# Causal block attention with a gated convolution: loads from two queues at the start, transposes evacuated between the two normalisations, the gates' work spread over the steps

## The chip, the core and the metric

One NeuronCore of a Trainium2 chip runs the whole kernel. The metric is device time in microseconds; the median of three runs stands for a kernel. Instructions run on five engines with a queue each: PE (TensorE, matmuls and transposes), DVE (VectorE), ACT (ScalarE), POOL (GpSimd) and SP (SyncE, which here only issues DMAs). ACT's queue issues some DMAs too.

## What is computed

Attention over 8 batches and 8 heads, 576 positions, head size 64, with a mask in blocks of 64 positions: a query sees its own block and all blocks before it. Its output, heads side by side (512 channels), goes through a gated unit: a causal convolution over 5 positions, per channel, gives the gate.

```python
scores = (q @ k.T) / sqrt(64)                  # masked by blocks of 64
attn   = softmax(scores) @ v                   # B, H, S, D
x      = attn, heads side by side              # B, S, 512
gate   = sigmoid(sum over k of conv_w[k] * xp[:, k:k+S])   # xp: x with 4 zeros ahead
out    = (gate * (x @ w_val)) @ w_out
```

## The kernel before

The 64 heads are worked in 32 pairs, p = 0 to 31; p belongs to batch b = p // 4. One trip of the loop at line 430 is called a step. The order of instructions on each engine is the order of the program: nothing is rescheduled (`tc.manual_schedule()`), and the framework only adds the waits.

A step p does, in the order of the program:

- **loads(p)**, line 388: on SP, q and k of pair p+4 (`load_qk1`), v of pair p+3 (`load_v1`), in some steps the last 64 positions ("tails") of q and k of a coming batch (`load_tails`) and of v (`load_vtail`), and in steps 1 to 4 the halves of w_val and w_out. The staging tiles of q, k and v have 4 buffers each.
- **casts(p)**, line 405: POOL turns float32 into float16: q and k of pair p+1 (from p = 5 on of pair p+2 as well, one step ahead), v of pair p, the tails, and in p = 6 and 7 the halves of w_out (`cast_w_out`).
- **s_tile(p, 0)** and **(p, 1)**, line 168: score matmuls into PSUM tiles S (two buffers), then exp on ACT into `pt`.
- **av(p-1)**, line 213: for each of the pair's two heads, 15 matmuls of the probabilities of the pair before with v into one PSUM bank, then on DVE a reciprocal of the sums (L234) and a multiplication (L235), which write `x16`.
- **trans(p+1)**, line 148: 8 transposes of the next pair's q and k on PE into bank 2, and one DVE copy to SBUF (`qkT`, L165).
- `permute_w_out` in p = 8 (two of them), 9 and 10, or an output tile from p = 11 on (`out(3)`: 4 matmuls of 512 columns in bank 3, a copy, a DMA).
- **s_tile(p, 2)** (here called S2) with its exp, and **mask(p)** (L204, L206): POOL writes zeros into the masked parts of `pt`. av(p) of the next step needs it.
- `s_last`, the scores among the tails, in some steps.
- from p = 5 on, with gs = p - 5: in even gs **conv(gs // 2)**, line 251, 80 small matmuls into one S tile and banks 0 and 1, then tanh on ACT (L266 for the two G banks, then L268 for the S tile).
- **xtrans(p-1)**, line 239: 5 transposes of `x16`, one DVE copy to `xts` (L246).
- in p = 5 and 6, two times `scale_w_val` (DVE, L379).
- from p = 6 on, two calls of **val**, line 271: 4 matmuls of x with w_val, then a DVE operation that applies the gate (`gv`, L282). The first uses bank 3, the second bank 0 or 2.
- `trans_tails` in some steps (PE, and a DVE copy L144).

[...] two S tiles of two banks each, and four single banks G0 to G3, which are given out by number. A bank is written again only when its last reader is done.

Step p = 0 is different: nothing is there to be normalised, and dummy matmuls (`warm(n)`, zeros by zeros) stand between the parts. Before the loop, the first loads, constants, the casts and the transposes of pair 0 are issued.

After the loop, the last av, the last val and conv and the output tiles that are left follow. Of the 36 output tiles, 21 are computed in steps 11 to 31 and 15 after the loop. In the tail, an output tile and a val alternate on PE.

Of the kernel before, what the change touches and what calls it, by code (L numbers as in the profile page):

```python
# [10 lines left out]
def kernel(  # L11
# [10 lines left out]
    nc = tc.nc  # L22
# [68 lines left out]
    def load_tails(b):  # L91
        t = p2.tile([128, 8, 64], fp32, tag="tlst", name="tlst")
        tl_st[b] = t
        for o, src in ((0, q), (64, k)):
            nc.sync.dma_start(out=t[o:o + 64, 0:8, 0:64],
                              in_=src[b, 0:8, 512:576, 0:64].rearrange("h s d -> s h d"))
# [5 lines left out]
    def load_v1(p):  # L102
        b, g = divmod(p, 4)
        t = p4.tile([128, 4, 2, 64], fp32, tag="vs1", name="vs1")
        for h in range(2):
            nc.sync.dma_start(
# [13 lines left out]
    def cast_qk(p, first=False):  # L120
# [4 lines left out]
        if first:  # L125
            nc.scalar.copy(out=o[:, 0:2], in_=s[:, 0:2])
# [86 lines left out]
    def av(p, banks):  # L213
# [3 lines left out]
        x = p2.tile([128, 5, 2, 64], fp16, tag="x16", name="x16")  # L217
        x16[p] = x
        for h in range(2):
            r = gbank(banks[h])  # L220
            for i in range(5):
                for j in range(i + 1):
                    if j == 4:
                        o = 64 * (4 * h + g)
                        l = pt4[b % 2][0:128].rearrange("p a s -> p (a s)")[:, o:o + 128]
                        w = v16t[b % 2][0:128, 2 * g + h, 0:65]
                    else:
                        o = 1280 + 64 * j if i == 4 else off[j] + 128 * i
                        l = pt[0:128, h, o:o + 128]
                        w = vv[0:128, j, h, 0:65]  # L230
                    mm(r[0:128, 65 * i:65 * i + 65], l, w, start=(j == 0), stop=(j == i))
            O = r[0:128, 0:325].rearrange("p (i d) -> p i d", d=65)
            rc = p2.tile([128, 5, 1], fp32, tag="rc", name="rc")
            nc.vector.reciprocal(out=rc[0:128], in_=O[:, :, 64:65])  # L234
            nc.vector.tensor_tensor(  # L235
                out=x[0:128, 0:5, h, 0:64], in0=O[:, :, 0:64],
                in1=rc[0:128].to_broadcast([128, 5, 64]), op=ALU.mult)
# [13 lines left out]
    def conv(n, banks=(None, None)):  # L251
# [13 lines left out]
        for row in (2, 3):  # L265
            nc.scalar.activation(out=t[0:128, row, 0:288], in_=rr[row][:, 0:288],  # L266
                                 func=AF.Tanh, bias=0.0, scale=0.5)
        nc.scalar.activation(out=t[0:128, 0:2, 0:288], in_=s[0:128, 0:2, 0:288],  # L268
# [119 lines left out]
    def loads(p):  # L388
        b, m = divmod(p, 4)
        if b + 2 < B and m == 2:  # L390
            load_tails(b + 2)
# [137 lines left out]
```

The softmax here doesn't subtract the row's maximum and nothing guards it: scores larger than these inputs give would overflow.

## Time and profile before

| | us |
|---|---|
| runs (three) | 198.04, 198.52, 198.67 |
| median | 198.52 |
| the profiled execution, its own time | 198.43 |
| its span in the trace | 196.6 |
| PE busy | 183.3 (93%) |
| DVE busy | 130.8 (67%) |
| ACT busy | 138.6 (71%) |
| POOL busy | 83.5 (42%) |

Times within the trace count from the start of the span. A step is found in the timeline by its score matmuls: the first ones of p = 1 start at 14.26 us, of p = 2 at 18.00, p = 3 at 21.74, p = 4 at 25.48, p = 6 at 34.27, p = 7 at 39.86, p = 8 at 46.32, p = 9 at 52.10, p = 10 at 57.19, p = 11 at 61.58, p = 12 at 67.19 and p = 13 at 72.10. In a timeline each line is: start in us, duration in us, engine, source line, operation, output<-input, shapes, count, and in brackets how long the engine had been idle and what ended that. A matmul's duration includes its way through the array, so that neighbours overlap; the distance between starts is what PE spends. In the view by windows each line has the window, its length, then busy time (and instructions) of PE, PEld (weight loads), DVE, ACT and POOL, the granted clock, the busy share of the DMA engines (above 1 when packets overlap) and GB/s.

### The profile page before, as it was taken

Reading aid. Unit: us, or ns where it says so; the run is one execution under the profiler, and the core shown is the slowest. Engines: PE = TensorE matmul, PEld = TensorE weight load, DVE = VectorE, ACT = ScalarE, POOL = GpSimd, SP = SyncE. Lnnn points to the kernel's source line nnn. Section 1 sums busy time; section 2 is a strip of 40 time slices with the busy share of each in tenths; the row PEclk is TensorE's granted clock in tenths of the full one; section 3 lists DMA queues with packets and bytes.
Section 4 is the critical chain, followed back from the end, with each engine's and each line's share of the span. In section 5 each row is a group of like instructions: output and inputs, shape, how many; then the busy total and the mean of one; then the engine's idle time right before and its main releaser. Section 6 shows DMA issues by size and latency. Waiting matters only on the chain.

```text
span 196.6 us, 8730 instructions
## 1 busy us (share of the span) xinstructions
PE 183.3 (93%) x3714; PEld 124.4 (63%) x3714; DVE 130.8 (67%) x286; ACT 138.6 (71%) x192; POOL 83.5 (42%) x168
## 2 busy tenths in 40 slices
PE   2999878779899999999999999999999999999992
PEld 1456656557577676667766677677767676755550
DVE  4346785897678686777686877768676868642451
ACT  4438778758699778877888878887988787635321
POOL 7363664596444554345434644464445422100000
PEclk9999999999999999999999999999999999999998
DMA  5999999999899568876887687977775111124445
GB/s 155 256 286 265 250 274 323 312 215 278 242 224 253 171 174 217 255 228 186 236 232 234 189 240 212 276 216 207 220 213 146 57 56 58 58 107 165 163 160 213
DMA packets 70337, 40.43 MB, mean 206 GB/s; under 512 B 48149, under 2 KB 64789, under 8 KB 70298
## 3 DMA queue, kind: packets, MB, share of 16 engines
q1 hardware_dynamic: 69872, 39.46, 73.8%
q8 instruction: 29, 0.48, 1.0%
q10 hardware_dynamic: 426, 0.40, 0.6%
q14 instruction: 10, 0.08, 0.2%
HBM read 30.42 MB, written 9.44 MB: 203 GB/s over the span
## 4 chain that ended last, share of the span: by engine, by line
PE 80%; DVE 10%; POOL 3%; ACT 2%; DMA 2%; issue 1%; POOLq 0%; SPq 0%; DVEq 0%; ACTq 0%
PE G L33 51%; PE S L33 18%; PE G L154 6%; PE G L244 5%; DVE qkT L165 3%; DVE x L235 3%; DMA vs<-in_v_dram 2%; POOL qk L129 1%; ACT pt L188 1%; PE G L141 1%; DVE w_val L379 1%; DVE rc L234 1%; DVE gv L282 1%; POOL v L134 1%; POOL pt L204 1%
## 5 line engine op out<-in xcount | busy, mean ns | idle before, releaser
L188 ACT ACTIVATE pt<-S 128x1024 f16<-128x1024 f32 x96 | 95.0, 1024 | 21.4 <-PE S L33 19.1
L204 POOL MEMSET pt<- 64x384 f16 x32 | 13.5, 423 | 74.0 <-ACT pt L188 73.9
L33 PE MATMUL G<-xt,w_val 128*128 128x288 f16 x256 | 37.9, 286 | 0.3 <-DVE qkT L165 0.2
L165 DVE COPY qkT<-G 128x1024 f16<-128x1024 f16 x31 | 37.7, 1215 | 0.2 <-PE G L154 0.2
L129 POOL CAST qk<-qks 128x1024 f16<-128x1024 f32 x31 | 32.9, 1061 | 10.9 <-DMA qks<-in_k_dram 7.7
L33 PEld LDWEIGHTS <-pt 128*128 128x128 f16 x960 | 31.2, 97 | 8.6 <-issue 4.0
L33 PE MATMUL G<-w_out,gv 128*128 128x512 f16 x144 | 36.5, 379 | 0.0
L33 PE MATMUL G<-v,pt 128*128 128x65 f16 x896 | 34.1, 194 | 1.7 <-DVE gv L282 1.3
L282 DVE SCALAR_TENSOR_TENSOR gv<-th,G 128x288 f16<-128x288 f32 x64 | 28.2, 453 | 10.7 <-PE G L33 9.0
L304 ACT COPY osb<-G 128x512 f32<-128x512 f32 x31 | 18.2, 586 | 23.8 <-PE G L33 22.0
L235 DVE TENSOR_TENSOR x<-G,rc 128x320 f16<-128x320 f32 x64 | 31.5, 492 | 2.2
L33 PEld LDWEIGHTS <-qkT 64*128 64x128 f16 x496 | 16.0, 94 | 22.9 <-issue 16.8
L33 PE MATMUL S<-qkT 64*128 64x512 f16 (+1 forms) x248 | 28.5, 301 | 2.1 <-DVE qkT L165 1.1
L33 PEld LDWEIGHTS <-w_val 128*128 128x128 f16 x256 | 24.2, 98 | 8.5 <-issue 0.9
L234 DVE RECIPROCAL rc<-G 128x5 f32<-128x5 f32 x64 | 12.2, 190 | 22.6 <-PE G L33 22.5
L246 DVE COPY xt<-G 128x576 f16<-128x576 f16 x32 | 14.6, 455 | 13.5 <-PE G L244 13.2
L154 PE MATMUL G<-ident,qk 128*128 128x128 f16 x256 | 20.1, 222 | 0.2 <-POOL qk L129 0.2
L134 POOL CAST v<-vs 128x512 f16<-128x512 f32 x32 | 19.9, 621 | 0.5 <-DMA vs<-in_v_dram 0.3
L33 PEld LDWEIGHTS <-gv 128*128 128x128 f16 x144 | 12.9, 98 | 9.9
L33 PE MATMUL G<-xt,DG 32*32 32x288 f16 x640 | 17.2, 288 | 0.0
L33 PE MATMUL S<-xt,DG 32*32 32x288 f16 x640 | 17.1, 287 | 0.0
L154 PEld LDWEIGHTS <-qk 128*128 128x128 f16 x256 | 15.4, 100 | 1.3 <-POOL qk L129 0.4
(58 smaller groups left out, 151.8 us busy)
## 6 DMA issues: line engine op xcount, KB each, us to landing
out_dram<-osb SPq DMA_DIRECT2D x35, 256.0 KB, 2.1
qks<-in_q_dram SPq DMA_DIRECT2D x32, 256.0 KB, 4.2
vs<-in_v_dram SPq DMA_DIRECT2D x64, 128.0 KB, 4.4
qks<-in_k_dram SPq DMA_DIRECT2D x31, 256.0 KB, 4.3
tlst<-in_q_dram SPq DMA_DIRECT2D x8, 128.0 KB, 4.8
tlst<-in_k_dram SPq DMA_DIRECT2D x8, 128.0 KB, 4.6
vtst<-in_v_dram SPq DMA_DIRECT2D x8, 128.0 KB, 4.8
w_st<-in_moe_w_val_dram SPq DMA_DIRECT2D x2, 512.0 KB, 6.3
```

Source lines behind the costliest of these rows:

```text
L33: nc.tensor.matmul(out=out, lhsT=lhsT, rhs=rhs, start=start, stop=stop, skip_group_check=True)
L129: nc.gpsimd.tensor_copy(out=o, in_=s)
L134: nc.gpsimd.tensor_copy(out=v16s[p % NV][0:128, 0:4, 0:2, 0:64], in_=s)
L154: nc.tensor.transpose(out=r[:, o:o + 128], in_=t[0:128, c, 2 * i:2 * i + 2, 0:64], identity=ident16[0:128, 0:128])
L165: nc.vector.tensor_copy(out=o[0:128].rearrange("p i (s n) -> p i s n", n=4), in_=src)
L188: nc.scalar.activation(out=pts[p % NPT][0:128, 0:2, 512 * t:512 * t + 512], in_=s[0:128, 0:2, 0:512], func=AF.Exp, bias=0.0, scale=0.125)
L204: nc.gpsimd.memset(pt[64:128, 0:2, 0:1536].rearrange("p h (t s) -> p h t s", t=3)[:, :, :, 0:64], 0.0)
L234: nc.vector.reciprocal(out=rc[0:128], in_=O[:, :, 64:65])
L235: nc.vector.tensor_tensor(out=x[0:128, 0:5, h, 0:64], in0=O[:, :, 0:64], in1=rc[0:128].to_broadcast([128, 5, 64]), op=ALU.mult)
L246: nc.vector.tensor_copy(out=xts[b % NX][0:128, g, 4:4 + SEQ], in_=r[:, 0:SEQ])
L282: nc.vector.scalar_tensor_tensor(out=gv[u][0:128, x, bi, hf, 0:288], in0=t[0:128, x, 0:288], scalar=1.0, in1=r[0:128, 0:288], op0=ALU.add, ...
L304: nc.scalar.copy(out=o[0:128], in_=r[0:128, 0:512])
```

## The change

Start. `load_tails(0)` and `load_v1(0)` are issued right behind the first q and k; the k part of the tails and both DMAs of v(0) go to ACT's DMA queue. `conv_nat` goes from ACT's queue to SP's, behind v(2). The first cast of q moves from ACT to DVE. The zeros for the dummy matmuls are written earlier.

Steps 0 to 4 get a loop of their own. Step 0 has fewer dummies and does trans(1) right after S2(0); conv_weights moves to p = 2. In steps 1 to 4 the transposes of `x16` are done two pairs behind instead of one, ahead of av (`x16` gets three buffers), and the program has the normalisation of head 0, av of head 1, trans(p+1), then the normalisation of head 1, so that DVE's copy of `qkT` stands between the two normalisations.

Loads and casts. The q and k tails of batch 2 are loaded in p = 4, behind v(7), instead of in p = 2 ahead of pair 6; they are cast and transposed in p = 6 instead of 4. `s_last(2)` goes from p = 6 to p = 8. The casts of w_out stand behind the mask in p = 7 and 8 instead of ahead of it in p = 6 and 7.

Gates. For p < 13 ("early") there is no output tile; the first val of a step takes its place, ahead of S2, and both val use bank 3. All four `scale_w_val` are in p = 6, two ahead of the first val and two after xtrans. The four `permute_w_out` are at the end of p = 9, 10, 11 and 12, in bank 2. In early steps conv's tanh takes the S tile first. Output tiles begin with p = 13.

```diff
         for o, src in ((0, q), (64, k)):
-            nc.sync.dma_start(out=t[o:o + 64, 0:8, 0:64],
+            (nc.scalar if b == 0 and o else nc.sync).dma_start(
+                              out=t[o:o + 64, 0:8, 0:64],
...
-    def load_v1(p):
+    def load_v1(p, eng=None):
...
         if first:
-            nc.scalar.copy(out=o[:, 0:2], in_=s[:, 0:2])
+            nc.vector.tensor_copy(out=o[:, 0:2], in_=s[:, 0:2])
             nc.vector.tensor_copy(out=o[:, 2:4], in_=s[:, 2:4])
...
-    def av(p, banks):
+    def av(p, h, bank):
...
+    def norm(p, h, bank):
+        if h == 0:
+            x16[p] = p3.tile([128, 5, 2, 64], fp16, tag="x16", name="x16")
+        O = GT[bank][0:128, 0:325].rearrange("p (i d) -> p i d", d=65)
+        rc = p2.tile([128, 5, 1], fp32, tag="rc", name="rc")
+        nc.vector.reciprocal(out=rc[0:128], in_=O[:, :, 64:65])
+        nc.vector.tensor_tensor(
+            out=x16[p][0:128, 0:5, h, 0:64], in0=O[:, :, 0:64],
+            in1=rc[0:128].to_broadcast([128, 5, 64]), op=ALU.mult)
+
+    def avs(p, banks):
         for h in range(2):
...
+            av(p, h, banks[h])
+            norm(p, h, banks[h])
...
-        for row in (2, 3):
...
+        for part in ((0, 2, 3) if score_first else (2, 3, 0)):
...
     load_qk1(0)
+    load_tails(0)
+    load_v1(0, nc.scalar)
...
-    nc.scalar.dma_start(out=conv_nat[0:5, 0:512], in_=moe_conv_w[:, :])
-    load_tails(0)
     make_identity(nc, ident)
+    wz = const([128, 512], fp16, "wz")
+    nc.vector.memset(wz[0:128], 0.0)
...
     load_v1(2)
+    nc.sync.dma_start(out=conv_nat[0:5, 0:512], in_=moe_conv_w[:, :])
...
-        if b + 2 < B and m == 2:
+        if b + 2 < B and m == 2 and b > 0:
             load_tails(b + 2)
...
-        if p == 0:
-            load_tails(1)
+        if p in (0, 4):
+            load_tails(1 + p // 4)
...
+    def tails(p):
+        if p in (3, 6):
+            return p // 3
+        return p // 4 + 1 if p > 4 and p % 4 == 0 and p + 4 < NP else None
...
-        if p in (6, 7):
-            cast_w_out(p - 6)
+        if tails(p):
+            cast_tails(tails(p), nc.gpsimd)
...
+    for p in range(LAG):
         loads(p)
         casts(p)
         s_tile(p, 0)
         s_tile(p, 1)
         if p == 0:
-            warm(3)
+            warm(2)
             trans_tails(0, 0)
...
+            s_tile(0, 2)
+            mask(0)
+            trans(1, 2)
+            warm(2)
+            s_last(0)
+            warm(4, 3)
+            continue
+        if p > 1:
+            xtrans(p - 2, 3)
+        av(p - 1, 0, 0)
+        norm(p - 1, 0, 0)
+        av(p - 1, 1, 1)
+        trans(p + 1, 2)
+        norm(p - 1, 1, 1)
         s_tile(p, 2)
         mask(p)
+        if p == 1:
+            warm(2, 3)
+        if p == 2:
+            conv_weights()
+        if tails(p):
+            trans_tails(tails(p), 0)
+        if p == 4:
+            s_last(1)
+
+    for p in range(LAG, NP):
+        gs = p - LAG
+        cv = gs % 2 == 0
+        early = p < 13
+        h = gs - 1
+        loads(p)
+        casts(p)
+        s_tile(p, 0)
+        s_tile(p, 1)
+        if p == LAG:
+            xtrans(p - 2, 3)
+        avs(p - 1, (0, 1) if cv else (1, 0))
+        if p < NP - 1:
+            trans(p + 1, 2)
+        if p == 6:
+            scale_w_val(0)
+            scale_w_val(1)
+        if not early:
+            out(3)
+        elif gs > 0:
+            val(h // 2, 2 * (h % 2), 3)
+        s_tile(p, 2)
+        mask(p)
+        if p in (7, 8):
+            cast_w_out(p - 7)
+        if p == 8 or (p % 4 == 2 and p > 6 and p + 2 < NP):
             s_last((p + 2) // 4)
...
         if cv:
-            conv(gs // 2, (0, 1))
...
+            conv(gs // 2, (0, 1), early)
+        xtrans(p - 1, 2 if cv else 0)
+        if p == 6:
+            scale_w_val(2)
+            scale_w_val(3)
         if gs > 0:
...
+            if not early:
+                val(h // 2, 2 * (h % 2), 3)
+            val(h // 2, 2 * (h % 2) + 1, 3 if early else 0 if cv else 2)
             if h % 2 == 1:
                 complete(h // 2)
-        if p == 8:
-            permute_w_out(1, 1)
...
+        if 9 <= p <= 12:
+            permute_w_out(p - 9, 2)
+        if tails(p):
+            trans_tails(tails(p), 1)
```

## The prediction

> **What bounds the kernel now.** I read four views in this order: the page's slices, busy time by windows, the timelines of POOL, DVE and PE one engine at a time, and the landing times of single DMAs. The page shows where there is room.
>
> ```profile
> PE   2999878779899999999999999999999999999992
> DMA  5999999999899568876887687977775111124445
> ```
>
> A slice is 4.9 us. PE is full from the twelfth slice on: the last 140 us only repeat what PE has to do, and a change pays only if PE is further ahead when this stretch begins. DMA is full in slices 2 to 9, exactly where PE has its gaps. The windows say the same with numbers:
>
> ```profile
> 8.00:12.00 4.00, 4.00 (x38) 2.29 (x33) 0.64 (x3) 2.96 (x3) 2.68 (x5) 1.00 1.20 251
> ...
> 28.00:32.00 4.00, 3.12 (x70) 2.29 (x67) 2.53 (x6) 3.29 (x4) 2.60 (x5) 1.00 1.12 323
> 32.00:36.00 4.00, 3.09 (x110) 1.88 (x107) 3.44 (x7) 3.34 (x7) 2.38 (x4) 1.00 1.09 316
> ...
> 40.00:44.00 4.00, 2.70 (x82) 1.99 (x86) 3.58 (x9) 2.20 (x3) 3.75 (x6) 1.00 0.89 198
> ```
>
> The columns are PE, PEld, DVE, ACT, POOL, clock, DMA share, GB/s. A DMA share above 1.0 from 3 to 40 us means a backlog: loads land in the order of issue, as fast as the engines allow. "PE 4.00" in 8 to 12 us is largely warm-up filler (11 of p=0's 16 dummy matmuls). What the backlog does is in POOL's timeline:
>
> ```profile
> 30.15 1.04 POOL L129 CAST qk<-qks 128x1024 f16<-128x1024 f32 x1
> 33.56 1.04 POOL L129 CAST qk<-qks 128x1024 f16<-128x1024 f32 x1 [2.37 <-DMA qks<-in_k_dram]
> 34.55 0.62 POOL L134 CAST v<-vs 128x512 f16<-128x512 f32 x1
> 35.23 0.57 POOL L204 MEMSET pt<- 64x384 f16 x1
> ...
> 38.30 1.04 POOL L129 CAST qk<-qks 128x1024 f16<-128x1024 f32 x1 [2.08 <-DMA qks<-in_k_dram]
> ```
>
> This is step p=5: the casts of pairs 6 and 7, then v, then the mask, in one queue. Pair 7 is wanted only in step 6, but POOL stands 2.37 us for it, and av(5) waits for the mask behind it (PE resumes at 35.85). Steps 5 to 7 thus already run at the pace of the loads. Later, DVE's order counts; step p=10:
>
> ```profile
> 58.46 0.20 DVE L234 RECIPROCAL rc<-G 128x5 f32<-128x5 f32 x1 [0.71 <-PE G L33]
> ...
> 59.73 1.22 DVE L165 COPY qkT<-G 128x1024 f16<-128x1024 f16 x1
> 60.86 0.45 DVE L246 COPY xt<-G 128x576 f16<-128x576 f16 x1
> 61.22 0.92 DVE L282 SCALAR_TENSOR_TENSOR gv<-th,G 128x288 f16<-128x288 f32 x2
> ```
>
> With av(9) starting at 57.73, the qkT evacuation ends at 60.95: 3.2 us after the start of av, in every step.
>
> **What the Trainium skill says.** "DMA: Bandwidth & Descriptors", section "Issuing engines are not separate DMA queues": loads issued from several engines run on the same 16 DMA engines and interleave, and a second queue saves only the sequencer's issue time. The shares above 1.0 agree that the engines, not SP, are short. "PSUM — Partial Sum Buffer", "PSUM bank collisions raise a hardware error": two engines may not be on one bank at once, so a bank is handed over only when its reader is done. The trace agrees: DVE's L160 stood 1.8 us for ACT's L159 on the other half of the same bank. "TensorE: Matmul & The Clock Gate", Part 1: the clock is halved until some 3.4 us of activity. The first four warm-up matmuls took 1.89 us, three at 8.18 us only 0.82, which agrees.
>
> **Part 1, the start (p=0).** q on DVE instead of ACT: DVE's half (0.43) can run while k is awaited (4.68), the ACT cast (0.62) goes; wz is cleared earlier, so the warm-ups no longer stand ahead of trans(0). S(0) comes about 0.5 earlier (7.63 now). The three DMAs moved to ACT's queue (k tail, two of v) free 1.8 us of issue on SP (0.62 + 1.21) and let vtail and pair 2 be issued earlier, which a full DMA gives no faster; conv_nat, 10 KB, goes to SP behind v(2), long ahead of its use in p=2. Bytes ahead of pair 1 grow by up to v(0) (256 KB, 0.9 us at 280 GB/s), so the cast of pair 1 (7.86 now) moves by 0 to +1.2. trans(1) follows it at once instead of standing at 12.31 behind conv_weights (1.05 us) and 11 dummies. Cast at 9.0, trans 10.1, qkT copy (1.23) to 12.0: S(1) at 11 to 12 instead of 14.26. **Lead 2.2 to 3.3 us**, with the clock perhaps still halved in part of it.
>
> **Part 2, steps 1 to 4.** Moving qkT ahead of the second normalisation frees it 0.63 us (L234+L235), but trans ends only 0.65 after av, and xtrans (0.31) now stands before av: DVE's loop S, av, qkT stays at 0.54+0.31+0.92+0.65+1.22 = 3.65 us against 3.74. It does not bind alone: S2, exp (0.51+1.03), mask (0.66), cast of q and k (1.10), trans (0.55) closes at 3.85 to 3.9 us (S2 at 16.27, 20.12, 23.97, 27.88), on PE, ACT and POOL, and is not touched. **Gain 0 to 0.1 a step; I take 0.** conv_weights in p=2 costs 1.05 us on PE and 1.0 on DVE, in their 0.8 us of slack a step: at most 0.3, taken as 0. The tanh order costs nothing by itself: the S bank comes free 0.7 earlier, row 3 as much later, and av of the next step waits up to 0.2 for it (a term below).
>
> **Part 3, loads and casts.** On SP the q and k of tails(2) move from ahead of pair 6 to behind v(7). By single landings, w_val lands at 19.61+7.0 = 26.6, the tails at 28.2: 1.6 us of DMA (their bytes alone at 250 GB/s would be 1.05, the low end). Pair 7's k, now 27.63+5.8 = 33.4, lands at 31.8. POOL: cast to 32.9, v to 33.5, mask to 34.1; av(5) at 34.05 instead of 35.85. **This is where the lead of part 1 is handed back**: whatever steps 0 to 4 gained, POOL waits for pair 7, and 1.8 us remain. Moved past each other on POOL: the cast of tails(2) (0.62) goes from p=4 to p=6, ahead of mask(6); its load, now behind v(7), lands at about 38.9, the cast ends at 39.5, before mask(6) is due (S2(6) at 38.4 plus 2.15). The casts of w_out (1.24, 1.05) leave their place ahead of mask(6) and mask(7), which was 41.14 and 44.88, for one behind mask(7) and mask(8); what waits behind them there, the cast of pair 10, has a step to spare. s_last(2) (0.21 on PE, 0.6 on ACT) goes from p=6 to p=8, with the same slack.
>
> **Part 4, step 6.** Before, two of the four scalings of w_val ran at 34.75 in DVE's idle time. Now all four are in p=6, and val(0,0) stands on PE before S2(6). DVE after av(5): first rc at 34.8, both normalisations 1.27, qkT 1.2, scale 0.67: PE waits until 37.9, S2(6) is at 38.4 (now 37.48). Then second scale 0.67, gv 0.42, xt 0.42 (with 0.3 of waiting for xtrans), two scales 1.4, gv 0.42, kt 0.4 for the tails that now also sit here: 41.9. av(6) needs kt's bank for its second head: 42.0, trans(8) at 42.4 against 42.69. Behind it PE is dense to S(8): trans 0.55, val 0.49, S2 and norm wait 0.8, conv 1.15, xtrans 0.31, val 0.49. S(8) at 45.7 instead of 46.32. **Lead L = 0.6 us.**
>
> **Part 5, steps 8 to 12.** Both val of a step now use bank 3. The first one's gv is queued on DVE behind qkT, so it ends at av+3.2+0.45, and the second val starts at av+3.7. In an even-p step PE has only av 0.92, trans 0.55, val 0.49, S2 0.24, xtrans 0.31 (and s_last 0.21) until then, so it idles about 1.0. Length: 0.54+3.7+0.49, plus tail transposes or permute 0.32 each, plus 0.1 to 0.2 for tanh's row 3: 5.2, 5.05, 5.35 for p=8, 10, 12. Odd p, with conv: 4.69 of PE work, permute 0.32, 0.15 until xt has left bank 2: 5.15. Sum 25.9. Before: S from 46.32 to 72.10, 25.8, with the same four permutes (two of them in p=8, with 0.7 of stall at 51.1), and **with two output tiles in it that the new version has not done** (p=11, 12). These go to the end: their four matmuls are 0.87 us (181.05 to 181.92), and PE is dense there, **+1.7 us**.
>
> **Sum.** -0.6 (lead) +0.1 (steps 8 to 12) +1.7 (two tiles later) = +1.2; I take +1.1, as the last-but-one tile fills 0.1 to 0.2 of a wait at 189.2. Against the profiled execution's own 198.43 (span 196.6 and 1.8 around it) that is 199.5. It is 0.1 below the median of the runs, 198.52, which I neglect.
>
> **The rivals.** *The lead survives* (faster): if the DMA engines take the early loads better from two rings, or pair 7's wait is shorter than its issue order says, steps 5 to 7 keep 2.5 to 3 us. Then 198.4+1.8-2.9 = 197.3. It decides from L = 1.8 at S(8); beyond that the change gains. For it: PE idles 3.4 us from 32 to 52; against: DMA shares of 1.09 to 1.12 there, and one queue's order. *It nets out* (same): L about 1.6, because scaling fits in POOL's wait, or the even steps idle 0.5 instead of 1.0: 198.5. *Deeper loss* (slower): no lead at S(8), and the permutes' ACT copies (0.58 each in bank 2) delay exp and trans in p=10 to 12 by 0.4 in two of the steps: 198.4+1.8+0.8 = 201.0.
>
> **Chances.** Forecast 0.45 (198.9 to 200.3), lead survives 0.25, nets out 0.2, deeper loss 0.1. Some 0.3% (0.6 us) is what a measurement can tell from no change. Faster 0.25, same 0.2, slower 0.55. The range leaves out a tenth on each side: 197.0 to 200.8; the forecast's own is 198.9 to 200.3.
>
> **What would show it.** Right: S(1) at 11 to 12; POOL's cast of pair 7 after a DMA wait of 3 us or more, ending near 33; in p=6 a PE wait of some 2 us ahead of val; in p=8, 10 and 12 PE waits on DVE's gv of about 1 us; PE again dense from p=13, with S(13) 0.5 earlier than 72.1 or later still, and 17 output tiles after the last step instead of 15. Wrong: pair 7 landing before 31; S(8) before 44.5; even steps under 4.8 us.

## The result, and the profile after

The change made the kernel slower by 1.3%: 201.39 us median (200.44 to 204.52) against 198.51, ratio 1.0133, 95% interval 1.0086 to 1.0180. The ratios here and below leave out any execution over 1.5% slower than the fastest of its kernel (of these four, 204.52); the medians hold all. A second measurement gave 201.93 against 198.76, 1.0176 (1.0122 to 1.0229). The forecast was 199.5 and its range ended at 200.8: the direction held, the size did not. The profiled execution took 201.78 (span 200.0), 3.35 more than that of the kernel before.

The slices of the page again, with the row of the clock, and the row of the queue that brings TensorE its program:

```profile
PE   3899778598998789999999999999999999999992
PEclk9999999969999999999999999999999999999999
DMA  6999999999989922877888687977684111144456
...
q8 instruction: 29, 0.48, 1.0%
```

PE is full from the sixteenth slice on, before from the twelfth. The ninth slice (40 to 45 us) has a clock of six tenths; the kernel before had none there. Busy time by windows (PE, PEld, DVE, ACT, POOL, clock, DMA share, GB/s):

```profile
8.00:12.00 4.00, 3.70 (x41) 1.82 (x38) 1.58 (x2) 3.46 (x4) 2.76 (x5) 1.00 1.18 261
28.00:32.00 4.00, 3.78 (x137) 2.86 (x137) 2.99 (x7) 3.31 (x5) 1.59 (x3) 1.00 1.07 316
32.00:36.00 4.00, 2.85 (x80) 2.04 (x60) 1.87 (x6) 3.30 (x6) 2.15 (x4) 1.00 1.07 272
36.00:40.00 4.00, 1.90 (x24) 1.32 (x25) 3.31 (x7) 0.80 (x1) 2.21 (x3) 0.96 0.96 276
40.00:44.00 4.00, 4.00 (x53) 2.96 (x51) 2.70 (x9) 2.16 (x3) 2.40 (x4) 0.62 1.19 203
```

From 36 to 40 us TensorE works 1.9 of 4 us; from 40 to 44 it looks full, but at 0.62 of the clock: the same matmuls last 1.6 to 1.7 times as long. TensorE's waits from 3 us on (total, times, longest) say what stands there, and name nothing for two of them:

```profile
PE G L33 <- DVE w_val L387: 2.4, 1, 2.4
...
PE G L33 <- DVE gv L291: 1.7, 2, 0.9
PE S L33 <- issue: 1.1, 1, 1.1
...
PE G L33 <- issue: 0.9, 1, 0.9
```

"issue" is time in which the engine waited for nothing that the profile shows. In TensorE's timeline the longer one lies within the eight matmuls of s_last in step 8:

```profile
49.06 0.22 PE L33 MATMUL S<-kt 64*128 64x64 f16 x4
50.40 0.23 PE L33 MATMUL S<-kt 64*128 64x64 f16 x4 [1.11 <-issue]
```

The other (0.95 us) is ahead of the last matmul of the convolution in step 11, at 66.69. POOL in p=5, and DVE in p=10:

```profile
28.81 1.04 POOL L130 CAST qk<-qks 128x1024 f16<-128x1024 f32 x1
32.01 1.04 POOL L130 CAST qk<-qks 128x1024 f16<-128x1024 f32 x1 [2.16 <-DMA qks<-in_k_dram]
33.00 0.62 POOL L135 CAST v<-vs 128x512 f16<-128x512 f32 x1
33.67 0.41 POOL L205 MEMSET pt<- 64x384 f16 x1
```

```profile
59.34 1.22 DVE L166 COPY qkT<-G 128x1024 f16<-128x1024 f16 x1
60.47 0.45 DVE L291 SCALAR_TENSOR_TENSOR gv<-th,G 128x288 f16<-128x288 f32 x1
60.83 0.45 DVE L253 COPY xt<-G 128x576 f16<-128x576 f16 x1
61.65 0.46 DVE L291 SCALAR_TENSOR_TENSOR gv<-th,G 128x288 f16<-128x288 f32 x1 [0.37 <-PE G L33]
```

Both are as forecast: pair 7 cast to 33.0 and the mask behind it, the first gv queued behind qkT, the second only after another val. Where the steps start in TensorE's timeline, us:

| kernel | S(1) | S(6) | S(8) | S(13) | S(13) to the end of the span |
|---|---|---|---|---|---|
| before | 14.26 | 34.27 | 46.32 | 72.10 | 124.5 |
| forecast | 11 to 12 | | 45.7 | 71.6 | 124.5 + 1.7 |
| changed | 12.36 | 32.79 | 46.32 | 73.65 | 126.35 |
| changed, second profile | 12.54 | 32.96 | 47.06 | 73.64 | 126.36 |

### The profile page after: what moved, and what is told of

Same layout as the page of the kernel before. It is cut to its first block, busy times and chain, and to the rows that moved or that the text cites. A ratio compares the mean times of both kernels' runs of the same rounds, so it can differ in the third digit from the quotient of the medians.

```text
span 200.0 us, 8704 instructions
## 1 busy us (share of the span) xinstructions
PE 182.6 (91%) x3704; PEld 124.1 (62%) x3704; DVE 130.9 (65%) x287; ACT 138.3 (69%) x191; POOL 82.9 (41%) x168
## 4 chain that ended last, share of the span: by engine, by line
PE 79%; DMA 5%; DVE 5%; POOL 4%; ACT 3%; issue 2%; SPq 0%; POOLq 0%; DVEq 0%; ACTq 0%
PE G L33 48%; PE S L33 18%; PE G L155 7%; PE G L251 5%; DMA vs<-in_v_dram 4%; DVE qkT L166 2%; POOL qk L130 2%; ACT pt L189 2%; DMA qks<-in_q_dram 2%; POOL v L135 1%; PE G L142 1%; DVE gv L291 1%; DVE qk L127 0%; DVE qk L161 0%; DVE w_val L387 0%
## 5 line engine op out<-in xcount | busy, mean ns | idle before, releaser
L33 PE MATMUL G<-xt,w_val 128*128 128x288 f16 x256 | 38.9, 287 | 4.1 <-DVE w_val L387 2.4
L291 DVE SCALAR_TENSOR_TENSOR gv<-th,G 128x288 f16<-128x288 f32 x64 | 28.4, 453 | 13.1 <-PE G L33 9.1
L33 PEld LDWEIGHTS <-pt 128*128 128x128 f16 x960 | 32.0, 98 | 7.0 <-issue 3.6
L33 PE MATMUL G<-v,pt 128*128 128x65 f16 x896 | 34.6, 195 | 0.8 <-POOL pt L205 0.7
```

What stands on the lines that cost most here:

```text
L33: nc.tensor.matmul(out=out, lhsT=lhsT, rhs=rhs, start=start, stop=stop, skip_group_check=True)
L291: nc.vector.scalar_tensor_tensor(out=gv[u][0:128, x, bi, hf, 0:288], in0=t[0:128, x, 0:288], scalar=1.0, in1=r[0:128, 0:288], op0=ALU.add, ...
```

## The experiments

My theory after the traces: the arithmetic of the tiles and of the gv waits held, and what came on top is the halved clock, waits for TensorE's own program, and a second late load behind w_val. Rivals: the terms of the sum were mis-sized, or the first five steps lost what the start won. Times are medians; the ratio is to the kernel before on the same chip.

### The unnamed waits: moving the blocks of the program

```diff
 def warm(n, bank=1):
-    for _ in range(n):
-        mm(GT[bank][0:128, 0:512], wz[0:128, 0:128], wz[0:128])
+    for _ in range(4 * n):
+        mm(GT[bank][0:128, 0:128], wz[0:128, 0:128], wz[0:128, 0:128])
```

> The changed kernel with each dummy matmul of 512 columns made into four of 128: the same columns on TensorE in the start, but 96 more TensorE instructions (48 weight loads, 48 matmuls) ahead of step 1. Nothing after the start is edited. In the trace of the changed kernel TensorE stood twice for nothing that the profile names, 1.11 us at 49.3 in step 8 and 0.95 us at 65.7 in step 11. Theory F (instruction fetch): the queue that brings TensorE's program moves 29 blocks of 16 KB, which is 256 instructions each; the two stalls sit 3 x 256 instructions apart, right behind a block that had landed only 0.2 to 0.4 us earlier. If so, 96 more instructions move the block boundaries: the stalls at these two places go, and any new ones stand 96 instructions earlier, near 47.1 in step 8 or 58.4 in step 10, or none; the time falls by 0 to 2 us to 199.5 to 201.5. Rival R (a wait that belongs to the program, such as an unnamed semaphore at s_last and at the end of the convolution): both stalls stay at the same instructions with the same lengths, and the time stays within 0.5 us of 201.4.

Measured 201.53, 1.0148 (1.0105 to 1.0191). Both waits are gone from their places: s_last in step 8 and the convolution in step 11 run through. Two smaller ones are new, 0.42 us at 34.3 and 0.21 at 89.3, neither where theory F had looked for them. Counted in the trace, the two waits of the changed kernel stand behind 1472 and 2240 TensorE instructions: 3 x 256 apart. The queue q8 brings 29 blocks, and TensorE's 3704 matmuls and 3704 weight loads are 28.9 times 256. **The twenty profiles of this study hold 29 such waits ("issue", TensorE, 3 to 190 us); they stand behind 960, 1472, 1984, 2240, 3264 or 4544 instructions, all multiples of 256 apart, and none stands anywhere else.** Theory F holds for the cause. What the waits gave back can't be read from the time: the profiled execution lost elsewhere (S(1) at 14.19, the clock halved from 40.98 to 44.39 us), and the median is that of the changed kernel.

### Step 6: the scalings, the clock, the tails

**Scalings of x 0 and 1 back in p=5:**

```diff
-        if p == 6:
-            scale_w_val(0)
-            scale_w_val(1)
...
-        if p == 6:
-            scale_w_val(2)
-            scale_w_val(3)
+        if p in (5, 6):
+            scale_w_val(2 * p - 10)
+            scale_w_val(2 * p - 9)
```

> The changed kernel with the first two scalings of w_val in p=5, as in the kernel before, so that TensorE doesn't stand 2.4 us for them in p=6. Theory A (the scaling is what p=6 loses): S(7) moves from 40.5 to about 38.5 and the clock is not halved; 1.5 to 2.5 us less, 199 to 200. Theory B (the tails of batch 2 stand right behind it): val(0,0) starts at 35.7 and S2(6) at 36.2, but POOL has the cast of the tails ahead of mask(6) and their k lands near 39, so the tail transposes in p=6 wait until about 39.7 and av(6) until the mask at 40.5; S(7) at 40.2 to 40.5, the clock still halved for 3.4 us, and only 0 to 0.6 us less: 200.8 to 201.4.

Measured 201.26, 1.0133 (1.0106 to 1.0159). S(7) is at 40.63: theory B. One wait replaced another, the cast of the tails, with mask(6) behind it:

```profile
39.63 0.61 POOL L116 CAST tl<-tlst 128x512 f16<-128x512 f32 x1 [1.69 <-DMA tlst<-in_k_dram]
40.31 0.57 POOL L205 MEMSET pt<- 64x384 f16 x1
```

It was wrong on the clock, which stayed up here; steps 6 and 7 took 11.24 instead of 13.53. But the start was 1.56 later and three waits for the program took 2.4, so the time hardly moved.

**Nine dummies ahead of val(0,0), the wait left in:**

```diff
         elif gs > 0:
+            if p == 6:
+                warm(9, 3)
             val(h // 2, 2 * (h % 2), 3)
```

> The changed kernel with nine dummy matmuls of 512 columns ahead of val(0,0) in p=6, in the bank that val then overwrites: they fill about 1.9 of the 2.4 us in which TensorE waits for the scaled w_val, and delay nothing. Theory C (the idle stretch halves the clock, and the halved clock is what turns my lead of 0.6 us at S(8) into none): no slice with a halved clock, S(7) at the same 40.5, av(6) 0.65 a head instead of 0.95, S(8) at 45.2 to 45.6 instead of 46.3, and 0.6 to 1.1 us less in the end. Rival (the clock costs nothing, since step 7 waits on other engines): S(8) stays at 46.3 and the time within 0.3 us of 201.4.

Measured 200.35, 1.0099 (1.0073 to 1.0125): 0.7 or 1.5 us less than the changed kernel by its two ratios, with matmuls that compute nothing. No slice of steps 6 and 7 has a halved clock, S(7) to S(8) took 5.07 instead of 5.81, and the page's clock row is clean:

```profile
PEclk9999999999999999999999999999999999999998
```

S(8) itself was at 47.31, since S(1) was at 14.30 and step 6 held a wait of 1.12 us for the program: my place for it was wrong, the 0.7 us of the step right.

**Scalings in p=5, tails cast and transposed in p=7:**

```diff
-        if p in (3, 6):
+        if p in (3, 7):
             return p // 3
...
-            trans_tails(tails(p), 1)
+            trans_tails(tails(p), 2 if p == 7 else 1)
```

> The changed kernel with the first two scalings in p=5 and, besides, the cast and the transposes of the tails of batch 2 in p=7 instead of p=6 (their load stays where the change put it). Theory B: with both waits of p=6 gone S(7) is at about 38.3 instead of 40.5, the clock stays up, and S(8) at 43.5 to 44.5, against 46.3; what is late next is mask(7), behind POOL's cast of pair 9, which lands near 42. 1.5 to 2.5 us less than the changed kernel, 199 to 200. Rival (the lead is worth nothing further on, since the waits for gv in the even steps or the loads take it back): S(8) earlier, but S(13) within 0.5 us of 73.6, and the time within 0.5 us of 201.4.

Measured 200.74, 1.0103 (1.0065 to 1.0141); 199.54 in the profiled execution. Steps 6 and 7 took 10.75 (kernel before: 12.05), S(8) at 45.17 though S(1) came at 13.99, S(13) at 71.40 instead of 73.65. The direction is theory B's, the size is not: S(7) and S(8) were expected at 38.3 and 43.5 to 44.5 and came at 39.73 and 45.17, and by the ratios the version is 0.6 or 1.5 us below the changed kernel, where 1.5 to 2.5 were expected.

### The start

In the profiles above whose start is the changed kernel's, unedited, S(1) was at 13.9 to 14.3. The two timelines of TensorE, of the changed kernel and of the run with the early scalings:

```profile
8.33 0.89 PE L33 MATMUL G<-wz 128*128 128x512 f16 x2
...
10.64 0.59 PE L33 MATMUL G<-wz 128*128 128x512 f16 x2
...
12.36 0.61 PE L33 MATMUL S<-qkT 64*128 64x512 f16 x6
```

```profile
8.34 1.04 PE L33 MATMUL G<-wz 128*128 128x512 f16 x2
...
11.47 1.06 PE L33 MATMUL G<-wz 128*128 128x512 f16 x2
...
13.92 0.61 PE L33 MATMUL S<-qkT 64*128 64x512 f16 x6
```

The same two dummies take 0.59 us in one and 1.06 in the other: the full clock came at 8.9 us there and at 13.1 here. (The page's clock row doesn't show this: it has nines from the first slice on.)

**Five more dummies in the gaps of the start:**

```diff
-    warm(4)
+    warm(8)
     cast_qk(0, first=True)
     trans(0)
-    warm(2)
+    warm(3)
```

> The changed kernel with four more dummy matmuls ahead of the first transposes and one more behind them, in stretches where TensorE idles 1.8 and 0.55 us. In the profile shown of the changed kernel the full clock came at 8.9 us and S(1) at 12.36; in the four profiles since (two of them with edits in p=6 and p=7 only) it came at 13.1 to 13.9 and S(1) at 13.9 to 14.3. Theory H (the start lost its lead to the halved clock, since the gaps between its dummies, 16 against 20 before, break the run of activity): the full clock comes before 9 us and S(1) at 11.4 to 12.4; of the 1.6 to 2.5 us gained, the wait for pair 7, which lands near 32, takes all but 0.6 to 1.0, and the time is 200.2 to 201.0. Rival (S(1) is set by the load and the cast of pair 1): S(1) stays at 13.9 or later. Second rival (pair 7 takes all of it): S(1) early, S(6) at 34.3 as in the last four profiles, and the time within 0.3 us of 201.4.

(Its count of dummies is off: up to S(1) there are 14 in the changed kernel and 23 before.) Measured 202.32, 1.0183 (1.0143 to 1.0222): S(1) at 12.01, the clock full from 5.2 us, and yet nothing gained. S(6) at 32.43, av(5) waits 1.1 us for the mask behind pair 7, then TensorE stands in step 6 for w_val, and this time two windows of the clock, 6.8 us, were halved:

```profile
PE   7699776599898989999999999999999999999992
PEclk9999999579999999999999999999999999999999
```

S(7) came at 42.27. Being early only made the hole in step 6 longer; neither the theory's time nor the rival's came out.

### Parts of the change by themselves

**The second val of even steps in bank 2:** the permutes of p=10 and 12 go to bank 1, the tail transposes of p=12 to bank 0.

```diff
-            val(h // 2, 2 * (h % 2) + 1, 3 if early else 0 if cv else 2)
+            val(h // 2, 2 * (h % 2) + 1, (3 if cv else 2) if early else 0 if cv else 2)
```

> The changed kernel with the second val of the even steps in bank 2 instead of bank 3, so that it needn't wait for the first one's gv; the permutes of p=10 and 12 go to bank 1 and the tail transposes of p=12 to bank 0. Theory G (the waits for gv cost what they show): the three waits, 0.8 to 1.0 each in p=8, 10 and 12, go, steps 8, 10 and 12 take 0.3 to 0.6 less each, and the time is 200.0 to 200.6. Rival (DVE's own queue of normalisation, qkT, two gv and xt sets these steps, so the wait moves to the next step's first av): the three steps together gain under 0.3 us, and the time is 201.1 to 201.4.

Measured 201.73, 1.0106 (1.0074 to 1.0138). The steps 8, 10 and 12 took 4.61, 4.71 and 5.04, against 4.98, 5.07 and 5.40 in the run with the nine dummies, so 0.36 less each: the waits for gv, 0.46 to 0.88 us of idling, became waits of 0.27 to 0.52 for qkT. The steps are the theory's. The median, above both ranges, mixes in the clock. A halved window of 3.41 us takes 0.0085 off the mean granted clock of 200 us. Counted by that figure, of the 22 executions of this version six had no such window behind the first full clock (200.1 us in the mean), seven had one (201.3) and nine had two (203.0). **By this count a halved window cost 1.3 to 1.7 us.**

**Start and first five steps of the change, loads and gates of before** (tails of batch 2 loaded in p=2 and cast in p=4, everything from step 5 on as in the kernel before):

```diff
-        if b + 2 < B and m == 2 and b > 0:
+        if b + 2 < B and m == 2:
             load_tails(b + 2)
...
-        if p in (0, 4):
-            load_tails(1 + p // 4)
+        if p == 0:
+            load_tails(1)
```

> The start and the first five steps of the changed kernel; the loads and casts of the tails of batch 2 and everything from step 5 on as in the kernel before. Theory H (the start's lead is eaten by the halved clock, step 3 loses another 0.6 to POOL's cast beside DVE's DG): S(1) at 13.9 to 14.3, S(5) at 29.6 to 30.1 against 29.53, and 198.2 to 199.2. Rival (the first five steps do gain, and what is lost lies in the gates): S(1) near 12.4, S(5) near 28.1, and 196.8 to 197.8.

Measured 199.42, 1.0040 (1.0017 to 1.0063): this half alone gains nothing, it costs 0.4%. S(1) at 13.24 was between the two, S(5) at 29.49 against 29.53.

**Gates and tails of the change, start and first five steps of before** (against the changed kernel, whose start and first loop are put back as they were):

```diff
-    load_v1(0, nc.scalar)
...
-            nc.vector.tensor_copy(out=o[:, 0:2], in_=s[:, 0:2])
+            nc.scalar.copy(out=o[:, 0:2], in_=s[:, 0:2])
...
-        if p == LAG:
-            xtrans(p - 2, 3)
```

> The start and the first five steps of the kernel before, with the tails of batch 2 loaded and cast as in the changed kernel and everything from step 5 on as in it. If the loss lies in the gates: step 6 takes 7.3 to 7.8 us for its two waits, S(8) is at 46.5 to 47.5, the two output tiles add 1.85 us behind the last step, and the time is 200.6 to 202.0, as far from 198.5 as the whole change. Rival (a good part of the loss comes from the first five steps): 199.2 to 200.2. The waits for instructions can add or take 1 us in either case.

Measured 202.37, 1.0169 (1.0124 to 1.0213): the loss lies in the gates and the tails. S(1) at 14.26, S(6) at 33.85, step 6 took 9.0 us, with two halved windows, S(8) at 48.35.

**Output tiles and permutes where they were:**

```diff
-        early = p < 13
+        early = p < 11
...
-        if p in (7, 8):
-            cast_w_out(p - 7)
+        if p in (6, 7):
+            cast_w_out(p - 6)
...
-        if 9 <= p <= 12:
-            permute_w_out(p - 9, 2)
+        if p == 8:
+            permute_w_out(0, 2)
+        if 8 <= p <= 10:
+            permute_w_out(p - 7, 0 if p == 8 else 2)
```

> The changed kernel with the permutes of w_out in p=8 to 10 and output tiles from p=11 on, as in the kernel before (so val is early only up to p=10); the rest as in the change. My forecast's term was +1.7 for the two tiles moved behind the last step, +0.1 for the steps 8 to 12. If it holds: the stretch from S(13) to the end takes 124.5 instead of 126.35 us, steps 11 and 12 grow by 0.3 to 0.6 together since the two tiles fill waits there, and the time is 199.7 to 200.5. Rival (TensorE is dense there, and the tiles cost the same where they are now put): steps 11 and 12 grow by 1.7, and the time stays within 0.4 us of 201.4.

Measured 200.65, 1.0100 (1.0063 to 1.0138). From S(13) to the end 124.9 us instead of 126.35, and steps 11 and 12 took 10.46, against 10.54 in the run with the nine dummies: **in p=11 and 12 the two tiles cost nothing, behind the last step 1.4 us.** (The permutes that left these steps made part of the room; step 9, which took one more of them, lasted 5.37 instead of 5.14.)

### The whole with its waits mended

**Old gates, filled start, mended loads:**

```diff
         for i in (p + 1, p + 2):
-            if i < NP and i not in qkT and i not in qk16 and (p >= 5 or i == p + 1):
+            if i < NP and i not in qkT and i not in qk16 and (p >= 12 or i == p + 1):
                 cast_qk(i)
```

That line, with the filled start, goes on the first five steps with the gates of before; the tails of batch 2 are loaded in p=4, cast and transposed in p=7, their s_last in p=8.

> The changed start and first five steps with five more dummies in their gaps, the gates of the kernel before, and nothing that waits for a late load out of turn: the tails of batch 2 are loaded behind the v of pair 7 and cast and transposed in p=7 (their last scores in p=8), and POOL casts a pair two steps ahead only from p=12 on, so that mask(5) no longer stands behind pair 7. Theory K (the lead of the start is real, and was lost to POOL's standing for pair 7 and for the tails, and to the clock that TensorE's idling halved): S(1) near 12, S(6) near 32.0, S(8) at 42 to 44, no slice with a halved clock after the start, S(13) at 69 to 70.5, and 195.5 to 197 us, faster than both kernels. Rival L (the loads bind up to 50 us whatever the order): S(8) at 45.5 or later, S(13) within 0.5 us of 72, and 198 to 199 us.

Measured 196.41, 0.9884 (0.9847 to 0.9920), faster than both kernels; a repetition beside the changed kernel:

> The version with the old gates, the filled start and the mended loads once more, beside the changed kernel on one chip: 196.0 to 197.5 us, 0.6 to 1.3% below the kernel before, if its first result holds; within 0.3% of it if that was luck with the phase of the clock.

196.47, 0.9877 (0.9838 to 0.9917). In its profile S(1) is at 12.00, S(8) at 44.61, S(13) at 70.32, and mask(5) no longer stands behind pair 7:

```profile
28.45 1.04 POOL L130 CAST qk<-qks 128x1024 f16<-128x1024 f32 x1
29.43 0.62 POOL L135 CAST v<-vs 128x512 f16<-128x512 f32 x1
31.97 0.41 POOL L205 MEMSET pt<- 64x384 f16 x1 [1.92 <-ACT pt L189]
32.33 0.20 POOL L207 MEMSET pt<- 64x128 f16 x1
32.59 1.04 POOL L130 CAST qk<-qks 128x1024 f16<-128x1024 f32 x1
```

Theory K holds in the time, though S(8) came later than the 42 to 44 us expected; in the first profile the clock fell back at 11.8 us, S(1) came at 14.03, and that execution took 198.56.

**The mended loads alone, in the kernel before:** the line above, and

```diff
-        if b + 2 < B and m == 2:
+        if b + 2 < B and m == 2 and b > 0:
             load_tails(b + 2)
...
-        if p == 0:
-            load_tails(1)
+        if p in (0, 4):
+            load_tails(1 + p // 4)
...
-        if p % 4 == 2 and p > 2 and p + 2 < NP:
+        if p == 8 or (p % 4 == 2 and p > 6 and p + 2 < NP):
```

> The kernel before, its start and first five steps and gates as they are, with the loads mended only: tails of batch 2 loaded behind the v of pair 7, cast and transposed in p=7, their last scores in p=8, and no cast two steps ahead before p=12. If the lead of the changed first five steps is what made the faster versions faster: S(1) at 14.3, S(6) at 33.6 to 33.9, S(8) at 45 to 46, and 197.6 to 198.3 us. Rival (POOL's waits in steps 5 to 7 were the whole loss): S(8) at 43 to 44.5, and 196 to 197 us.

Measured 197.90, 0.9969 (0.9948 to 0.9990): 0.3% is the loads'; the other 0.9% (0.4% by the version below that has one more gap filled) is the early start that they no longer hand back.

**All waits of the changed kernel mended** by the edits shown, its gates kept and the tiles late; and then with the tiles from p=11 on:

> The changed kernel with each of its known waits mended: five more dummies in the start, scalings of x 0 and 1 in p=5, tails of batch 2 cast and transposed in p=7, no cast two steps ahead before p=12, the second val of even steps in bank 2. Theory K: S(8) at 42.5 to 44.5, the steps 8 to 12 together 24.8 to 25.3, S(13) at 68 to 69.5, the two output tiles moved to the end still cost 1.85 us there, and 196 to 197.5 us. Rival L (the loads bind): S(8) at 45.5 or later, and 199.5 to 200.5 us. Rival F (what remains is instruction fetch): clean waits, but 1 to 3 us of stalls at the block boundaries, and 198 to 200 us.

> The kernel with all waits mended (start filled, scalings in p=5, tails in p=7, no early cast, second val of even steps in bank 2) and, besides, the permutes in p=8 to 10 and the output tiles from p=11 on. Theory K: as the one with the tiles late, but with 1.85 us less at the end and up to 1.2 more in steps 11 and 12: S(8) at 42.5 to 44.5, S(13) at 68.5 to 70, and 195 to 196.5 us, the fastest of all. Rival L (loads bind): S(13) within 0.5 us of 72, and 198 to 199 us.

198.73, 0.9958 (0.9934 to 0.9982), and 197.30, 0.9898 (0.9855 to 0.9941). Both medians are above theory K's ranges. With the tiles late S(1) was at 14.72 (the clock fell back at 11.0 us) and S(8) at 46.37 in the profiled execution, 200.61; it has no wait for the program, so rival F, whose range the median fits, isn't what held it up. With the tiles early S(1) was at 11.85, S(8) at 43.82, S(13) at 69.54, 195.85 in that execution. Its steps 8 to 12 took 25.72, the kernel before 25.78: spreading the gates gains nothing in them even without its waits.

**The last gap of the start filled**, with old and with new gates:

```diff
             mask(0)
+            warm(4, 3)
             trans(1, 2)
```

> The version with the old gates and the mended loads, with four more dummies ahead of the transposes of pair 1, where TensorE idled 1.6 us in its profile (the clock fell back at 11.8 us, S(1) came at 14.03 and that execution took 198.56; the others of it 196.0 to 197.1). If the scatter is the clock falling back in the start: the clock stays up from its rise before 9 us on, S(1) at 12.0 to 12.6, S(8) at 43 to 44.5, and all executions lie within 0.8 us of each other near 196. Rival (the scatter is something else): the spread stays at 2 us or more.

> The version with all waits mended, new gates and tiles from p=11 on, with four more dummies ahead of the transposes of pair 1. With the clock up from before 9 us in every execution: S(1) at 11.8 to 12.5, S(8) at 43.5 to 44.5, S(13) at 69.3 to 70.3, and 195.8 to 196.6 us; against the old gates with the same start 0 to 0.5 less. Rival (the new gates cost something against the old ones once their waits are gone): 0.5 to 1.5 more than the old gates with the same start.

197.44, 0.9928 (0.9903 to 0.9952), and 197.28, 0.9924 (0.9906 to 0.9942). The clock stayed up in both profiles, with S(1) at 12.25 and 12.53, but the executions still lie between 195.9 and 198.4 and between 196.1 and 200.3: the clock in the start is not the whole scatter. Some of the rest is the clock all the same: of the 22 executions with the new gates four granted 0.988 to 0.991 and took 199.8 us in the mean, the other eighteen 0.996 or more and 197.1. Expected times and spread were missed; between the old gates and the new with the same start no difference shows.

### The clock kept up in the changed kernel

```diff
+        if p == 6:
+            warm(3, 3)
         avs(p - 1, (0, 1) if cv else (1, 0))
```

and the nine dummies ahead of val(0,0), and both fillings of the start.

> The changed kernel, all its waits left in, with dummies wherever TensorE idles long enough for the clock to fall: five in the gaps of the start, four more ahead of the transposes of pair 1, three ahead of av(5) and nine ahead of val(0,0) in step 6. If the halved clock is what my forecast left out: no halved clock from 9 us to the end, S(1) near 12.2, S(7) near 40.5, S(8) at 45.3 to 45.9 (forecast 45.7), and 199.2 to 200.0 us, the forecast's 199.5. Rival (instruction fetch and the second wait of step 6 make up the difference): the clock is up and the time is 200.6 to 201.4 all the same.

Measured 200.35, 1.0101 (1.0065 to 1.0137), halfway between theory and rival. The clock is full from 5.1 us to the end, S(7) at 40.16 and S(8) at 45.23, the lead 1.1: as forecast, and better. Step 8 then took 6.70 us instead of 5.2:

```profile
PE G L142 <- POOL tl L116: 1.6, 2, 1.4
```

The tails of batch 3 had landed at 46.2, but their cast is queued on POOL behind that of pair 10, whose k landed at 48.68 and whose cast began at 48.83. It is the wait of step 5 over again, one load later: POOL stands for a pair that is not yet needed, and what is needed stands behind it.

**The changed kernel itself once more:**

> The changed kernel itself once more, unedited, for more executions and another profile. If the clock's windows have no fixed phase to the kernel's start: S(1) anywhere from 12.3 to 14.3, one or two windows of 3.41 us with a halved clock in steps 6 and 7 or none, waits for nothing named only at multiples of 256 TensorE instructions from the two already seen, and executions scattered over 200 to 202.5 us with a median of 200.8 to 201.8. If the first profile was the rule: S(1) at 12.4 again and all executions within 0.6 us of each other.

201.93, 1.0176 (1.0122 to 1.0229); executions from 201.2 to 203.8, scattered more widely and higher than expected, but with S(1) at 12.54 near the first profile's. One halved window in steps 6 and 7, and waits for the program behind instructions 960 and 1472 (0.8 and 1.4 us).

## Why the prediction was wrong

The sum was -0.6 (lead at S(8)) + 0.1 (steps 8 to 12) + 1.7 (two tiles later), taken as +1.1; the profile showed 0.0 + 1.55 + 1.8 = +3.35. Two things failed in it: the lead of part 4, which left out what the wait in step 6 does to the clock, and the sum itself, which had no term for TensorE's waits for its program.

- **Part 1, the start: size wrong.** S(0) came 0.26 us earlier (7.37), not 0.5. "With the clock perhaps still halved in part of it" stood there without a price. Up to S(1) the change has 14 dummies where there were 23, with gaps of 1.8 and 0.55 us between them; the full clock came anywhere from 8.9 to 13.9 us (before: 7.2 to 8.9), and S(1) from 12.36 to 14.30 in the eight profiles of this start with its dummies whole. Their mean is 13.3, a lead of 1.0, not 2.2 to 3.3; the 12.36 of the first profile is the luckiest of them.
- **Part 2, the first five steps: right that they gain nothing, wrong at conv_weights.** S(1) to S(6) took 20.43 in the changed kernel, 20.01 before. Step 3, behind conv_weights (put at 0.3 at most and taken as 0), grew from 3.74 to 4.41: POOL's cast of pair 4 took 1.60 us instead of 1.04 while DVE built DG (0.82) beside it, and the transposes waited 0.41 for it. The rest of the 0.67 isn't traced, and no run moved conv_weights. "GPSIMD Engine Reference" in the Trainium skill, section "8. Key points", says that POOL shares its SBUF interfaces with DVE and contends with DVE instructions of two SBUF inputs, as DG is; the 1.60 agrees.
- **Part 3, loads and casts: right**, to 0.2 us: pair 7 cast at 32.01, v at 33.00, av(5) at 34.14 (forecast 34.05).
- **Part 4, step 6: this step failed.** The wait was right (val(0,0) at 38.10, forecast 37.9), but what it does to the clock was left out. TensorE had worked little since 35.7, and from 39.66 to 43.07 its clock was halved: av(6) took 0.8 us a head instead of 0.47, trans(8) came at 43.10 instead of 42.4, and the lead of 0.6 was gone. With dummies in the wait and the clock up, step 6 began alike (32.63 us, 32.79 in the changed kernel) and S(8) came at 45.23. (The terms listed behind trans(8) add up to 3.8 us, not to the 3.3 that S(8) at 45.7 needs; by luck TensorE took 3.2.) Steps 6 and 7 took, less the unnamed waits in them, 11.5 and 12.3 us in the two runs whose clock was held up by dummies, 12.9 to 13.5 with one halved window (the changed kernel twice, blocks moved, tiles back), 13.8 to 14.2 with two (filled start, second val in bank 2, gates alone). Between profiles whose step 6 began within 0.4 us of each other that is **1.1 to 1.5 us for one window and 1.9 for two**. "TensorE: Matmul & The Clock Gate", Part 1, which I cited for the start, has the rule for step 6 too: the clock falls back after about a window of 3.4 us of idling, and the windows run freely. On the windows the runs agree: the halved stretches were 3.41 or 6.83 us, and full ones 30.72 and 157.01, 9 and 46 windows. On the idling they don't: TensorE stood for 2.42 us at most, and was still busy for 1.56 of the 3.41 us ahead of the fall; the last section has the measured line.
- **Part 5, steps 8 to 12: right where TensorE had its program.** 5.2, 5.15, 5.05, 5.15, 5.35 were forecast; the run with nine dummies took 4.98, 5.14, 5.07, 5.14, 5.40, in sum 25.7 (forecast 25.9). The changed kernel took 5.34, 5.14, 5.07, **6.37**, 5.40: the excess is the two waits for the program, 1.11 and 0.95 us of idling. Step 11 lost 1.23 us by its wait, step 8 only 0.36, since its wait for gv went. No step of the prediction had them: it read the DMA as full in slices 2 to 9, but the row shows eight or nine tenths up to the thirteenth, 64 us (in the changed kernel up to the fourteenth, 70 us), and both waits fall in that stretch. (The 0.15 for tanh was added in p=8 alone, though p=10 and 12 also follow a convolution; no step shows it.) The two tiles cost 1.8 in all behind S(13) (forecast 1.7), of which 1.4 came back when they were put back.

One reading was off, without weight in the sum: of the 1.8 us that DVE's L160 stood, 1.1 passed until the transposes ended at 6.23 us, and only 0.6 until ACT's copy did at 6.85.

Of the rivals, "deeper loss" came nearest in time (201.0) and in one half of its mechanism (no lead at S(8)), but for another reason; the permutes delayed nothing that shows in steps 10 and 12. "The lead survives" became true only once the loads were mended too.

What stays open is how the 1.9 us between forecast and median divide. The run with the clock kept up (granted 0.997 or more in all six executions) was 0.3 to 0.75% faster than the changed kernel, which is 0.6 to 1.5 us, and its median of 200.35 is still 0.85 above the forecast. Of the changed kernel's ten executions, by the granted clock, one had no halved window behind its start (201.20 us), six had one, two had two and one had three. The waits for the program differ from one execution to the next (2.1 and 2.2 us in the two profiles of the same kernel). That blocks land late because the DMA engines are full was not tried; it is argued from the landings alone.

## What to carry to other kernels

An idle stretch of TensorE like the 2.4 us of step 6 costs twice: its length, and the window or two of halved clock behind it, 1.1 to 1.9 us here. Before counting a lead, follow each in-order queue to the first item that is not yet needed: here POOL stood for pair 7, then for the tails, then for pair 10, and each handed lead back until casts were put in order of need. The two output tiles cost nothing in steps with waits, and 1.4 us of their 1.7 where TensorE is dense.

## What the runs showed of the hardware

TensorE's program comes by DMA in blocks of 256 instructions, and TensorE can run out of it. In the changed kernel the block of step 8 began to move 3.2 us after the block boundary ahead of it was crossed, landed at 48.88, and TensorE, which had reached the boundary at 49.1, went on at 50.4; the block of step 11 landed at 65.09, TensorE went on at 66.69. So it went on 1.5 to 1.6 us after the landing. In the kernel before, the three tightest blocks landed 1.4 to 1.7 us ahead of their boundary, and nothing waited. After 75 us, with a DMA share of 0.63 in the changed kernel instead of 1.03 from 44 to 68 us, 17 of its 18 blocks began to move within 1.1 us, and of the 29 waits only 3 lie there. A convolution alone is 160 instructions in 0.8 us. Dummies that fill a wait thus also shift the boundaries; what a shift is worth in the median isn't shown (201.53 us with the blocks moved, 201.39 without).

The clock fell back by the busy share of a window. Laid end to end from each profile's first full clock, windows of 3.41 us at the full clock number 1049 in the twenty profiles (the last 7 us of each left out). In the nine after which the clock was halved TensorE was busy for 31 to 51% of the window; in each of the other 1040 it was busy for 57% or more. Two windows by that view, ahead of the fall in the changed kernel, and the emptiest that kept the clock, in the run with the clock kept up:

```profile
36.25:39.66 3.41, 1.56 (x22) 1.16 (x23) 2.72 (x5) 0.46 (x1) 2.07 (x3) 1.00 0.98 286
49.48:52.89 3.41, 1.94 (x28) 1.15 (x28) 1.25 (x3) 1.28 (x3) 3.29 (x7) 1.00 0.92 240
```

The line here is thus near half a window (busy time as the profile models it), and whether a wait of 2.4 us crosses it depends on where it lies on the windows, which the program doesn't choose.
